# Inputs of head pairs 2 and 3 loaded ahead of the weights, and new operation lengths in a kernel's own list scheduler

## The chip, the core and the metric

The kernel runs on one core of one Trainium2 chip. The core has five engines with their own instruction queues: TensorE (PE; its weight loads are listed apart as PEld), VectorE (DVE), ScalarE (ACT), GpSimd (POOL) and SyncE (SP). SP computes nothing here; it issues nearly all DMA transfers. The metric is the device time of one launch in microseconds (us); lower is better. The median of three runs of the kernel before is 600.06 us (597.63 to 600.74).

## The reference

Gated linear attention (a state per head, decayed by alpha and fed by k and v, read by q), then the real part of a 2D Fourier transform of the result, added to it, then a layer norm and a feed-forward layer of ReLU type. The weights come as float64, the rest as float32. Cut to what matters:

```python
# q, k, v, alpha: (4, 8, 768, 48), alpha in 0.8 .. 1.0
for t in range(768):
    state = alpha[:, :, t, :, None] * state + np.einsum('bhd,bhe->bhde', k[:, :, t], v[:, :, t])
    y[:, :, t] = np.einsum('bhd,bhde->bhe', q[:, :, t], state)
x = y.transpose(0, 2, 1, 3).reshape(4, 768, 384)
u = x + np.real(np.fft.fft(np.fft.fft(x, axis=1), axis=2))
un = (u - u.mean(-1, keepdims=True)) / np.sqrt(u.var(-1, keepdims=True) + 1e-6)
out = u + np.maximum(un @ w_ch1, 0.0) @ w_ch2      # w_ch1 (384, 1536), w_ch2 (1536, 384)
```

## The kernel before

**Work and stages.** There are 4 batches (b = 0 to 3) of 4 head pairs, so 16 pairs, counted 0 to 15 in the code and in this text. For each batch there is a front (attention of its four pairs, then mixing) and a feed-forward part over two blocks of 384 tokens.

Attention of a pair is `attn_stages` (L609), stages s1 to s7 and a last one. s1 takes the products of the decays: `products` (L615) runs two scans of 112 x 768 elements on DVE over the tile `al` (alpha), with a few tiny operations between them: a copy of every 64th decay into `d1` (trace: COPY d<-al), a reciprocal, a copy of reciprocals into `d1` (COPY d<-rec), and the product `mt`. s2 and s3 multiply by k and q out of the tile `kq` (`times`, L643, on DVE or POOL). s4 transposes k (PE) into `kt`; s5 (pairs 0 to 6, float32) or s5r (from pair 7, in split float32r, tiles `qs`) makes the masked products of q and k (PE, ACT; the mask is an affine_select on POOL, tile `w`); s6 makes the states `tt` (PE, ACT, two DVE scans of 288); s7 makes y out of the masked products, `vn` (v) and `tt` on PE. The last stage is `combine` (L766): sums and differences of halves and thirds of the sequence, on POOL, with two steps on DVE.

Mixing is `mix_stages` (L783): `f2` (L799) folds the 384 columns on DVE, with nine tiny column copies per batch (COPY w<-x or w<-w, 128 x 2 or 4; each on the flexible list 'fc', which names DVE alone); then two rounds of Fourier matmuls (`mk_s`, `mk_d`) with additions on DVE. `norm_stages` (L887) normalises and transposes a block. `ffn_stages` (L935) is the feed-forward part: for each block 12 steps, each with 9 matmuls of 128 x 384 to the hidden layer and 9 back; ACT and DVE split each hidden tile `h` between them. In the trace these matmuls are f<-x,wt and f<-wt,h; there are 1728 of them, 432 per batch.

**Weights.** float64 weights come in four groups g of three tiles `wt0` to `wt11` (`load_weights`, L577, four DMAs each). `wsplit` (L588) turns a tile into a high and a low float32r part, with DVE, ACT and POOL steps; 12 splits in all. Feed-forward of batch 0 walks the weights in parts of 6, 3 and 3 steps (groups 0 and 1, then 2, then 3).

**The order.** The program writes instructions down with a key each, and `Plan.emit` (L331) gives every engine a fixed order by list scheduling: at each step it takes, over all engines, the instruction that can start first by the plan's own clock, and among those of an engine that could start within a small window the one with the lowest key. The lengths that this clock uses come from `duration` (L289). An operation with a flexible engine list (L447: 'mul' is DVE or POOL, and so on) goes to the engine that ends it first, with some slack (L446). The hardware then runs each engine's list in that order; an engine whose next instruction is not ready waits, whatever else would be ready behind it. Keys: batch 0's attention from -600 (`order`, `front` L1012), its weights' splits KW = -505 and KW1 = -260, later splits KW2 = 515, mixing of batch 0 KF0 = -505, attention of batch 1 K1 = 515, feed-forward 500 up.

**Transfers.** All SP loads keep program order (`self.chain` in `add`). A load whose tile is still in use holds the SP queue. `kq` and `vn` have two tiles each (NQK, NVN, L39 and L40), `al` has four (NAL). `load_first` brings pair 0, then come pair 1 (L1088 on) and a second copy of pair 0's alpha for the range check (`check_first`); alpha of pair p + 2 is issued behind s1 of pair p (`front`), k, q and v of pair p + 2 behind s7 of pair p. The weight groups are issued behind the units of `order` counted by LG = (8, 22, 40, 52), the Fourier constants `cst` behind unit L1 = 35. PE runs filler matmuls on a tile of zeros (trace: f<-zero, L1099) in gaps that the plan sees in its first 120 us.

Of the kernel before, what the change touches and what calls it, by code (L numbers as in the profile page):

```python
# [26 lines left out]
C = 64  # L27
# [15 lines left out]
KW = -505.0  # L43
LG = (8, 22, 40, 52)
L1 = 35
MIX = (5, 2, 2, 3, 3)
# [68 lines left out]
class View:  # L115
    """A tile of the plan, or a part of one: the steps are replayed on the real tile."""

# [18 lines left out]
class Slot:  # L136
    """One tile as the program sees it; it gets a real tile of its tag when its first instruction is placed."""

# [5 lines left out]
class Rows:  # L144
    """Row numbers of an indirect DMA."""

# [29 lines left out]
class Plan:  # L176
    """Instructions written down in program order, then given an order on every engine by list scheduling."""

# [37 lines left out]
    def add(self, engines, name, args, kwargs):  # L216
        engine = engines[0]
        fns = {e: self.method(e, name) for e in engines}
        if self.direct:
            return fns[engine](*[real(a) for a in args], **{k: real(x) for k, x in kwargs.items()})  # L220
        op = Op(engines, fns, args, kwargs, self.key)
        n = len(self.ops)
        self.ops.append(op)
        named = [("out" if i == 0 and "out" not in kwargs else i, a) for i, a in enumerate(args)] + list(kwargs.items())
        op.free, op.fill = 1, self.fill
        op.bytes = None
        for k, a in named:
            if isinstance(a, Rows):
                a = a.view
            if isinstance(a, View):  # L230
                self.touch(n, op, a, k in ("out", "accum_out"))
                if k == "out":
                    op.free = self.region(a)[4]
                if k == 2:
                    op.moving = a
        op.name = name
        named = dict((str(k), a) for k, a in named)
        op.durs = {e: self.duration(op, named, e) for e in engines}
        if engine == "SP" and isinstance(named["out"], View):
            if self.chain is not None and self.chain not in op.deps:  # L240
                op.behind = self.chain
                op.deps.add(self.chain)
            self.chain = n
        if "dma" in name:
            op.wire = self.wire(named)
# [43 lines left out]
    def duration(self, op, named, engine):  # L289
# [3 lines left out]
        if engine == "PE":  # L293
            m = self.region(named["1"])[4]
            if op.name == "transpose":
                return max(m, self.region(named["2"])[4]) / 1200 + 0.002
            if str(named["1"].real(self.base(named["1"])).dtype).endswith("float32"):
                return max(m, n) / 600 + 0.004
            return n / 2400 + 0.003
        if engine == "ACT":  # L300
            pointer = 0.094 if any(isinstance(named.get(k), View) for k in ("bias", "scale")) else 0.0
            return (0.05 if self.psum(named.get("1")) else 0.093) + n / 1200 + pointer + (0.096 if "accum_out" in named else 0.0)
        if op.name == "memset":
            return n / (960 if engine == "DVE" else 1100) + 0.01
        if engine == "DVE":
            if op.name == "bn_stats":
                return 0.47
            if op.name == "reciprocal":
                return 0.07 + n / 160
            if isinstance(named.get("scalar1"), View):  # L310
                return 0.07 + n / 1200
            whole = "bitcast" in [s[0] for s in named.get("out", View(None)).steps]
            pointer = 0.06 if isinstance(named.get("scalar"), View) else 0.0
            return 0.07 + pointer + n / (1920 if whole and op.name == "tensor_scalar" else 960)
        return 0.126 + n / 1094 if op.name == "affine_select" else 0.15 + n / 477

    def psum(self, view):
# [13 lines left out]
    def emit(self):  # L331
# [11 lines left out]
        dge, wire = 0.0, 0.0  # L343
        order = []

        def start(op, e):
# [14 lines left out]
        while placed < len(ops):  # L361
# [39 lines left out]
            if op.name == "matmul" and self.idle and (op.args[0].tile.tag, op.args[0].tile.cell) == self.idle[3]:  # L401
                self.open = not op.kwargs["stop"]
            end = t + op.dur
            clock[op.engine] = end
# [41 lines left out]
SLACK = {'ACT': 2.0, 'DVE': 0.5, 'POOL': 5.0}  # L446
FX = {'comb': 'G', 'mul': 'VG', 'first': 'G', 'wm': 'VG', 'wd': 'VG', 'fold': 'V', 'ev': 'A', 'relu': 'A', 'un': 'V', 'hi': 'A', 'xh': 'A', 'er': 'AV', 'fc': 'V', 'kl': 'V'}  # L447
WINDOW = {'PE': 0.0, 'ACT': 0.15, 'DVE': 0.05, 'POOL': 0.5, 'SP': 0.0, 'DMA': 0.0}
# [3 lines left out]
def gla_mix_ffn(ctx: ExitStack, tc: tile.TileContext, alpha, kq, v, w1, w2, consts, rowtab, out):  # L452
# [41 lines left out]
    def w3():  # L494
        return plan.tile("w3")

    def fixed(shape, name, dtype=F32):
        return plan.fixed(cp.tile(shape, dtype, name=name))

# [1 line left out]
    cst = fixed([P, CONST_W], "cst")  # L501
# [38 lines left out]
    def load_alpha(p):  # L540
        if p < B * NP2:
            t = plan.tile("al")
            loaded["al", p] = t
            SY.dma_start(t[0:CW, 0:S], alpha[p])

    def load_rest(p):
        if p < B * NP2:
            t, vn = plan.tile("kq"), plan.tile("vn")
            loaded["kq", p] = t
            loaded["vn", p] = vn  # L550
            SY.dma_start(t[0:CW], kq[p])
            SY.dma_start(vn, v[p])
# [54 lines left out]

# [1 line left out]
    def attn_stages(b, hp, i, mixed):  # L609
# [5 lines left out]
        def products(lo, hi):  # L615
            as_, Af, o = loaded["al", pair], e["A"], off(lo)
            d, chunks = d1[0:CW, lo:hi], slice(lo // C, hi // C)
            V.tensor_copy(d[:, 0::C], as_[0:CW, o : o + hi - lo : C])
            V.memset(as_[0:CW, o : o + hi - lo + 1 : C], 0.0)
# [5 lines left out]
            V.reciprocal(r, part[:, C - 1 :: C])  # L625
            V.tensor_copy(d[:, 2 * C - 1 :: 2 * C], r[:, 1::2])
            j0, j1 = max(lo // P - 1, 0), hi // P - 1
# [129 lines left out]

# [1 line left out]
    def early():  # L759
# [23 lines left out]
    def mix_stages(ytiles, zt, scr, us):  # L783
# [15 lines left out]
        def f2():  # L799
# [4 lines left out]
            for z, f in zip(zp, fp):  # L804
                ze, zo = f[:, :, 0 : HM + 1], f[:, :, HM:DM]
                E.tensor_add(ze[:, :, 1:HM], z[:, :, 1:HM], z[:, :, DM - 1 : HM : -1])
                FL["fc"].copy(ze[:, :, 0 : HM + 1 : HM], z[:, :, 0 : HM + 1 : HM])
                E.tensor_sub(zo[:, :, 1:HM], z[:, :, 1:HM], z[:, :, DM - 1 : HM : -1])
                g = [z[:, :, o : o + len(r)] for o, (r, _) in zip((0, HQ + 1, 2 * HQ + 1, 3 * HQ), GROUPS)]
                E.tensor_add(g[0][:, :, 0:HQ], ze[:, :, 0:HQ], ze[:, :, HM:HQ:-1])  # L810
                FL["fc"].copy(g[0][:, :, HQ : HQ + 1], ze[:, :, HQ : HQ + 1])
                E.tensor_sub(g[1][:, :, 0:HQ], ze[:, :, 0:HQ], ze[:, :, HM:HQ:-1])
                E.tensor_sub(g[2][:, :, 0 : HQ - 1], zo[:, :, 1:HQ], zo[:, :, HM - 1 : HQ : -1])
                E.tensor_add(g[3][:, :, 0 : HQ - 1], zo[:, :, 1:HQ], zo[:, :, HM - 1 : HQ : -1])
                FL["fc"].copy(g[3][:, :, HQ - 1 : HQ], zo[:, :, HQ : HQ + 1])
                for i in range(2):
# [67 lines left out]

# [1 line left out]
    def norm_stages(us, blk, res):  # L886
        e = {}  # L887

        def n1():
# [16 lines left out]
            if blk == 0:  # L906
                uw = [w3(), w3()]
                un = [uw[0][:, 0:DM], uw[0][:, DM:S], uw[1][:, 0:DM]]
# [22 lines left out]

# [1 line left out]
    def ffn_stages(us, blk, res, store, f0=0, f1=DFF // P):  # L933
# [56 lines left out]
    def batch(b):  # L990
# [5 lines left out]
        return mixed  # L996

    def front(b, us, ress):
        mixed = batch(b)
        sts = [attn_stages(b, hp, (b * NP2 + hp) % 2, mixed) for hp in range(NP2)]  # L1000

        def unit(hp, n):
            def f():
                if hp < NP2:
                    sts[hp][n]()
                    if n == 0:
                        load_alpha(b * NP2 + hp + 2)
# [4 lines left out]
        for hp in range(NP2):  # L1012
            order += [
                unit(hp, 3), unit(hp, 4), unit(hp + 2, 0), unit(hp, 5), unit(hp + 1, 1),
                unit(hp + 1, 2), unit(hp, 6), lambda hp=hp: load_rest(b * NP2 + hp + 2), unit(hp, 7),
            ]
# [19 lines left out]
    load_first()  # L1036
    load_alpha(1)
    load_rest(1)
    us, ress = [], [{}, {}]
    order, mixing = front(0, us, ress)  # L1040

    def extra(i):
        if i in LG:
            load_weights(LG.index(i))
        if i == L1:
            load_consts(1)

    plan.key = KCK
    check_first()
    write(order, -600.0, after=extra)  # L1050
    plan.key = KW
# [48 lines left out]
    with tc.manual_schedule():  # L1100
        plan.emit()
# [1 line left out]
    main_pool.close()  # L1103
# [101 lines left out]
def layout(q, k, v, alpha, moe_w_ch1, moe_w_ch2):  # L1205
    """The inputs as the launch takes them: heads in pairs with the features before the tokens, float64 as 8-byte words."""

# [18 lines left out]
def tokens(o):  # L1226
    """The blocks of the launch as the rows of the sequence: the second block holds the tokens from the end."""
    res = np.empty((B, S, DM), o.dtype)
# [19 lines left out]
```

## Time and profile before

| | before |
|---|---|
| median of three runs | 600.06 us (597.63 to 600.74) |
| the profiled execution, span from first to last instruction | 600.8 us |
| PE busy in the span | 543.5 us (90%) |
| DVE busy | 397.0 us (66%) |
| POOL busy | 214.1 us (36%) |
| ACT busy | 213.4 us (36%) |
| HBM traffic | 69 GB/s over the span |

The page gives no time of the profiled execution other than its span; it lies 0.7 us above the median and 0.1 us above the highest of the three runs, so that sums made in the trace can be set against the median directly. How to read it: a row of the timeline has start, length, engine, line, operation, tiles (out<-in), shapes, count, and in brackets the idle time before it and what ended that. Nearly all instructions have line L434, since `emit` records them; the tile names tell them apart. Tile numbers are left out, so `w` is any of the `w3` tiles, `x`, `h`, `qs`, `al` and `y` likewise. The windows view gives the busy time of each engine in a stretch, with the number of instructions, the clock granted to TensorE (1.00 is full speed) and the DMA rate.

### The profile page before, as it was taken

The numbers are of one execution on the slowest core, as the hardware profiler recorded it, in microseconds if no ns is written. First come the engines' busy times: TensorE is split into PE (matmuls) and PEld (weight loads), VectorE is DVE, ScalarE is ACT, GpSimd is POOL, SyncE is SP. The second block draws the span as 40 slices with busy tenths as digits, with TensorE's granted clock in tenths as the row PEclk, the third lists the DMA queues.
The fourth block names the chain that finished last, engine by engine and source line by source line (L and its number), as shares of the span: only waits on it lengthen the run. The fifth ranks groups of instructions, "written<-read, shape, count | busy, mean of one in ns | idle before, by whom it ended". The sixth has DMA issues, their size and how long they took to land. (4 is left out here: it accounts for less than half of the span.)

```text
span 600.8 us, 9105 instructions
## 1 busy us (share of the span) xinstructions
PE 543.5 (90%) x3470; PEld 523.2 (87%) x3470; DVE 397.0 (66%) x863; ACT 213.4 (36%) x442; POOL 214.1 (36%) x252
## 2 busy tenths in 40 slices
PE   7989588998779999787999989977999999999995
PEld 6878578897679998777999979977999999999995
DVE  7998999879955699896635991596635921412211
ACT  2657233575333313464622221444712121211110
POOL 3689794337526101395540040085740000000000
PEclk7568567689959999997979999987979999999999
DMA  8827291720014101143240110120010000100101
GB/s 219 280 74 278 67 321 50 247 67 0 2 35 130 48 0 41 44 130 92 67 140 6 40 47 0 41 67 21 1 55 26 33 8 1 40 1 1 40 1 44
DMA packets 16546, 42.16 MB, mean 70 GB/s; under 512 B 1904, under 2 KB 7088, under 8 KB 16496
## 3 DMA queue, kind: packets, MB, share of 16 engines
q1 hardware_dynamic: 15440, 39.08, 20.5%
q0 software_dynamic: 768, 2.36, 1.5%
q8 instruction: 29, 0.48, 0.4%
q14 instruction: 21, 0.17, 0.1%
q10 hardware_dynamic: 288, 0.07, 0.1%
HBM read 34.42 MB, written 7.08 MB: 69 GB/s over the span
## 5 line engine op out<-in xcount | busy, mean ns | idle before, releaser
L434 PE MATMUL f<-wt,h 128*128 128x384 f32 x864 | 179.5, 347 | 6.3 <-DVE h L434 3.3
L434 PE MATMUL f<-x,wt 128*128 128x384 f32 x864 | 179.7, 347 | 0.0
L434 PEld LDWEIGHTS f<-wt,h 128*128 128x128 f32 x864 | 154.2, 193 | 8.7 <-DVE h L434 4.5
L434 PEld LDWEIGHTS f<-x,wt 128*128 128x128 f32 x864 | 155.3, 193 | 0.6 <-issue 0.3
L434 DVE SCALAR_TENSOR_TENSOR h<-f,h 128x384 fp32r<-128x384 f32 x96 | 53.1, 553 | 128.9 <-ACT h L212 128.5
L212 ACT ACTIVATE h<-f 128x384 fp32r<-128x384 f32 x96 | 47.1, 491 | 192.4 <-PE f L434 181.4
L434 POOL TENSOR_SCALAR_AFFINE_SELECT w<-w 128x512 f32<-128x512 f32 (+1 forms) x64 | 48.8, 790 | 47.8 <-ACT w L434 47.8
L434 PEld LDWEIGHTS a<-vn,w 128*128 128x128 f32 x324 | 58.3, 251 | 7.4 <-POOL w L434 7.0
L434 PE MATMUL a<-vn,w 128*128 128x64 f32 x324 | 59.7, 326 | 5.4 <-POOL w L434 5.4
L434 POOL TENSOR_TENSOR sd<-y,y 128x288 f32<-128x288 f32 x32 | 30.8, 984 | 53.5 <-ACT y L434 52.3
L434 POOL TENSOR_TENSOR w<-w,rec 112x384 f32<-112x384 f32 (+1 forms) x17 | 17.8, 1049 | 87.2 <-DVE mt L434 83.2
L434 PE MATMUL a<-tt,w 112*128 112x96 f32 x134 | 40.5, 400 | 8.6 <-DVE tt L434 8.6
L434 DVE SCALAR_TENSOR_TENSOR qs<-w,hm,qs 112x384 fp32r<-112x384 f32 x36 | 24.7, 711 | 27.2 <-ACT qs L434 27.1
L434 ACT COPY w<-a 128x512 f32<-128x512 f32 (+6 forms) x58 | 25.9, 481 | 33.0 <-PE a L434 26.6
L434 DVE TENSOR_TENSOR_SCAN al<-al,d 112x768 f32<-112x768 f32 (+1 forms) x17 | 36.7, 2160 | 0.4
L434 DVE TENSOR_TENSOR y<-y,a 128x191 f32<-128x191 f32 (+2 forms) x96 | 28.7, 342 | 12.4 <-PE a L434 12.3
L434 PEld LDWEIGHTS a<-tt,w 112*128 112x128 f32 x134 | 28.0, 261 | 9.8 <-DVE tt L434 9.7
L434 PE MATMUL a<-qs,qs 112*128 112x256 f32 x162 | 31.6, 322 | 4.8 <-DVE qs L434 4.1
L434 POOL TENSOR_TENSOR w<-sd 128x96 f32<-128x96 f32 x64 | 35.7, 577 | 0.0
L434 PE MATMUL a<-cst,w 96*128 96x96 f32 (+10 forms) x267 | 33.7, 269 | 0.0
L434 PEld LDWEIGHTS a<-cst,w 128*96 128x96 f32 (+7 forms) x267 | 32.3, 169 | 0.9
L434 PEld LDWEIGHTS a<-qs,qs 112*128 112x128 f32 x162 | 26.1, 217 | 7.8 <-DVE qs L434 5.5
(124 smaller groups left out, 743.3 us busy)
## 6 DMA issues: line engine op xcount, KB each, us to landing
kq<-in_kq_dram SPq DMA_DIRECT2D x15, 672.0 KB, 7.5
wt<-in_w_dram SPq DMA_DIRECT2D x8, 768.0 KB, 9.6
al<-in_alpha_dram SPq DMA_DIRECT2D x15, 336.0 KB, 4.3
vn<-in_v_dram SPq DMA_DIRECT2D x16, 296.0 KB, 2.8
out_dram<-y SPq DMA_DIRECT2D x24, 192.0 KB, 1.9
wt<-in_w_dram SPq DMA_DIRECT2D x8, 384.0 KB, 6.3
scr<-y SPq DMA_DIRECT2D x4, 576.0 KB, 4.5
cst<-in_consts_dram SPq DMA_DIRECT2D x1, 832.5 KB, 5.2
```

Of the source, the lines that this page charges most:

```text
L212: return lambda out, x: e.activation(out, x, AF.Relu)
L434: op.ins = op.fns[op.engine](*[real(a) for a in op.args], **{k: real(x) for k, x in op.kwargs.items()})
```

## The change

Four things are changed.

1. Pairs 1, 2 and 3 (the second to the fourth) are loaded right behind pair 0: alpha, k and q, and v. k and q of pairs 2 and 3 go into the tiles `wt9` and `wt10`, v of both into `wt11`, which are those of weight group 3. Groups 0 and 1 and the Fourier constants are issued right behind, group 2 and 3 behind units 30 and 41 of the order. Behind pair 0 and 1 come k, q and v of pairs 4 and 5; from pair 4 on it is as before. Alpha of pair 4 on is issued from pair 2 on.
2. The lengths in `duration` are changed: longer for feed-forward matmuls, for strided float32 matmuls, for ACT, for the DVE scans; 0.02 us more for most DVE operations.
3. `emit` gets a model of DVE and POOL slowing each other: an operation with two wide SBUF inputs ("part") is lengthened by half of its overlap with the other engine's last operation, a tensor_scalar with fixed numbers ("whole") by all of it, and POOL's clock is pushed too.
4. The tiny copies in `products` and `f2` (70 in the trace before) become a DVE tensor_tensor, x or x on the bits (`same`). The normalised block 0 of batch 0 goes into two `qs` tiles instead of two `w3` tiles.

```diff
-LG = (8, 22, 40, 52)
-L1 = 35
+LG = (30, 41)
...
         op.durs = {e: self.duration(op, named, e) for e in engines}
+        op.port = self.port(op, named) if engine in ("DVE", "POOL") else None
...
             if str(named["1"].real(self.base(named["1"])).dtype).endswith("float32"):
-                return max(m, n) / 600 + 0.004
-            return n / 2400 + 0.003
+                slow = 1.65 if self.stride(named["2"]) > 16 else 1.0
+                return max(m, slow * n) / 600 + 0.004
+            return n / 2240 + 0.003
         if engine == "ACT":
             pointer = 0.094 if any(isinstance(named.get(k), View) for k in ("bias", "scale")) else 0.0
-            return (0.05 if self.psum(named.get("1")) else 0.093) + n / 1200 + pointer + (0.096 if "accum_out" in named else 0.0)
+            slow = 1.8 if self.stride(named["out"]) > 16 and n > 64 else 1.0
+            return (0.11 if self.psum(named.get("1")) else 0.14) + slow * n / 1200 + pointer + (0.25 if "accum_out" in named else 0.0)
...
+            if op.name == "tensor_tensor_scan":
+                return 0.1 + n / 480
             if isinstance(named.get("scalar1"), View):
-                return 0.07 + n / 1200
+                return 0.09 + n / 1200
...
-            return 0.07 + pointer + n / (1920 if whole and op.name == "tensor_scalar" else 960)
+            return 0.09 + pointer + n / (1920 if whole and op.name == "tensor_scalar" else 960)
...
+    def port(self, op, named):
+
+        if op.engine == "POOL":
+            return None if "dma" in op.name else "part"
+        if op.engine != "DVE" or op.name == "memset":
+            return None
+        inputs = [a for k, a in named.items() if k != "out" and isinstance(a, View)]
+        wide = [a for a in inputs if a.tile.tag not in ("a", "f1", "f2") and self.region(a)[4] > 1]
+        if len(wide) > 1:
+            return "part"
+        return "whole" if wide and op.name in ("tensor_scalar", "tensor_copy", "copy") and "scalar1" in named else None
...
+        held = {"DVE": (0.0, 0.0), "POOL": (0.0, 0.0)}
...
+            if op.port and op.engine in held:
+                other = "POOL" if op.engine == "DVE" else "DVE"
+                a, b = held[other]
+                both = max(0.0, min(b, t + op.dur) - max(a, t))
+                op.dur += (SHARE if op.port == "part" else 1.0) * both
+                if other == "POOL":
+                    clock[other] += SHARE * both
+                held[op.engine] = (t, t + op.dur)
...
+SHARE = 0.5
...
+    def same(out, x):
+        x = x.bitcast(I32)
+        V.tensor_tensor(out=out.bitcast(I32), in0=x, in1=x, op=ALU.bitwise_or)
...
+    def plain(t):
+        return t.rearrange("p c two n -> p (c two n)").bitcast(F32)
+
     def load_rest(p):
         if p < B * NP2:
-            t, vn = plan.tile("kq"), plan.tile("vn")
+            if p in (2, 3):
+                if p == 2:
+                    loaded["lent"] = plain(plan.tile("wt11"))
+                t = plain(plan.tile(f"wt{7 + p}")).rearrange("p (two s) -> p two s", two=2)
+                vn = loaded["lent"][:, (p - 2) * VW : (p - 1) * VW]
+            else:
+                t, vn = plan.tile("kq"), plan.tile("vn")
...
-            V.tensor_copy(d[:, 0::C], as_[0:CW, o : o + hi - lo : C])
+            same(d[:, 0::C], as_[0:CW, o : o + hi - lo : C])
...
-            V.tensor_copy(d[:, 2 * C - 1 :: 2 * C], r[:, 1::2])
+            same(d[:, 2 * C - 1 :: 2 * C], r[:, 1::2])
...
-                FL["fc"].copy(ze[:, :, 0 : HM + 1 : HM], z[:, :, 0 : HM + 1 : HM])
+                same(ze[:, :, 0 : HM + 1 : HM], z[:, :, 0 : HM + 1 : HM])
...
-                uw = [w3(), w3()]
+                uw = [plan.tile("qs").bitcast(F32) if state["start"] else w3() for _ in range(2)]
...
+    def rest_after(p):
+        if p < 2:
+            load_rest(p + 4)
+        elif p > 3:
+            load_rest(p + 2)
...
-                    if n == 0:
+                    if n == 0 and b * NP2 + hp > 1:
                         load_alpha(b * NP2 + hp + 2)
...
-    load_alpha(1)
-    load_rest(1)
+    for p in (1, 2, 3):
+        load_alpha(p)
+        load_rest(p)
...
     def extra(i):
         if i in LG:
-            load_weights(LG.index(i))
-        if i == L1:
-            load_consts(1)
+            load_weights(2 + LG.index(i))
...
+    plan.key = -600.0
+    load_weights(0)
+    load_consts(1)
+    load_weights(1)
     write(order, -600.0, after=extra)
```

More of the change, by code (lines that the diff above doesn't have):

```diff
@@ L309, in duration, with stride @@
                 return 0.07 + n / 160
+            if op.name == "tensor_tensor_scan":
+                return 0.1 + n / 480
             if isinstance(named.get("scalar1"), View):
-                return 0.07 + n / 1200
+                return 0.09 + n / 1200
             whole = "bitcast" in [s[0] for s in named.get("out", View(None)).steps]
             pointer = 0.06 if isinstance(named.get("scalar"), View) else 0.0
-            return 0.07 + pointer + n / (1920 if whole and op.name == "tensor_scalar" else 960)
+            return 0.09 + pointer + n / (1920 if whole and op.name == "tensor_scalar" else 960)
         return 0.126 + n / 1094 if op.name == "affine_select" else 0.15 + n / 477
+    def stride(self, view):
+        ap = view.real(self.base(view))
+        return abs(ap.ap[-1][0]) * mybir.dt.size(ap.dtype)
+    def port(self, op, named):
[8 more added lines that the diff above has]
+        return "whole" if wide and op.name in ("tensor_scalar", "tensor_copy", "copy") and "scalar1" in named else None
     def psum(self, view):
@@ L446 @@
 SLACK = {'ACT': 2.0, 'DVE': 0.5, 'POOL': 5.0}
-FX = {'comb': 'G', 'mul': 'VG', 'first': 'G', 'wm': 'VG', 'wd': 'VG', 'fold': 'V', 'ev': 'A', 'relu': 'A', 'un': 'V', 'hi': 'A', 'xh': 'A', 'er': 'AV', 'fc': 'V', 'kl': 'V'}
+FX = {'comb': 'G', 'mul': 'VG', 'first': 'G', 'wm': 'VG', 'wd': 'VG', 'fold': 'V', 'ev': 'A', 'relu': 'A', 'un': 'V', 'hi': 'A', 'xh': 'A', 'er': 'AV', 'kl': 'V'}
+SHARE = 0.5
 WINDOW = {'PE': 0.0, 'ACT': 0.15, 'DVE': 0.05, 'POOL': 0.5, 'SP': 0.0, 'DMA': 0.0}
@@ L810, in f2 @@
                 E.tensor_add(g[0][:, :, 0:HQ], ze[:, :, 0:HQ], ze[:, :, HM:HQ:-1])
-                FL["fc"].copy(g[0][:, :, HQ : HQ + 1], ze[:, :, HQ : HQ + 1])
+                same(g[0][:, :, HQ : HQ + 1], ze[:, :, HQ : HQ + 1])
                 E.tensor_sub(g[1][:, :, 0:HQ], ze[:, :, 0:HQ], ze[:, :, HM:HQ:-1])
@@ L814, in f2 @@
                 E.tensor_add(g[3][:, :, 0 : HQ - 1], zo[:, :, 1:HQ], zo[:, :, HM - 1 : HQ : -1])
-                FL["fc"].copy(g[3][:, :, HQ - 1 : HQ], zo[:, :, HQ : HQ + 1])
+                same(g[3][:, :, HQ - 1 : HQ], zo[:, :, HQ : HQ + 1])
                 for i in range(2):
@@ L1014, in front @@
                 unit(hp, 3), unit(hp, 4), unit(hp + 2, 0), unit(hp, 5), unit(hp + 1, 1),
-                unit(hp + 1, 2), unit(hp, 6), lambda hp=hp: load_rest(b * NP2 + hp + 2), unit(hp, 7),
+                unit(hp + 1, 2), unit(hp, 6), lambda hp=hp: rest_after(b * NP2 + hp), unit(hp, 7),
             ]
```

## The prediction

> **What bounds the kernel now.** I read the windows view first, with cuts at the start of the feed-forward part, at the end of the weight splits, and where DVE fills up again.
>
> ```profile
> core 0: us, PE busy (x) PEld busy (x) DVE busy (x) ACT busy (x) POOL busy (x), PEclk, DMA share, GB/s
> 0.00:119.88 119.88, 99.77 (x778) 91.99 (x779) 108.91 (x233) 55.56 (x111) 79.17 (x89) 0.68 0.62 193
> 119.88:172.00 52.12, 42.21 (x237) 39.48 (x236) 48.08 (x65) 27.37 (x46) 28.28 (x22) 0.89 0.06 20
> ...
> 234.00:280.00 46.00, 35.97 (x233) 32.38 (x232) 42.10 (x74) 22.03 (x49) 24.62 (x23) 0.97 0.22 65
> ...
> 119.88:593.20 473.32, 442.69 (x2690) 430.56 (x2690) 286.55 (x629) 157.84 (x331) 134.89 (x163) 0.94 0.13 39
> ```
>
> Two regimes are to be seen. Up to 172 us DVE is busy for 108.91 + 48.08 = 157 of 172 us (91%), so DVE sets the pace there; PE's busy time of the first stretch holds filler matmuls. From 119.88 on PE carries the feed-forward and what is left of attention and mixing. It loses 473.32 - 442.69 = 30.6 us idle, and at a mean clock of 0.94 another 0.06 x 473.32 = 28.4 us: 59 us that aren't work at full speed. In 234 to 280, with DVE 42.10 of 46 us busy, PE is idle for 10. The chain of waits, near the end of the run:
>
> ```profile
> 480.92 33.55 PE f L434 x192
> ```
>
> 192 matmuls in 33.55 us are 0.175 us each, back to back; nothing in this change makes one shorter. So only three things can move the end: DVE work up to 172 us, PE's idle time behind that, and the clock. What PE waits for from 119.88 on (total us, times, longest), the three largest rows:
>
> ```profile
> PE a L434 <- DVE tt L434: 7.1, 3, 3.3
> PE a L434 <- DVE al L434: 6.9, 2, 6.5
> PE a L434 <- DVE qs L434: 4.1, 3, 2.9
> ```
>
> These 18.1 of the 30.6 us (60%) are attention matmuls that stand in PE's fixed order ahead of their operands.
>
> **The change, part by part.** *Small copies.* Those up to 172 us, grouped by form, and a small product with two SBUF inputs of the same stage:
>
> ```profile
> L434 DVE COPY w<-x 128x2 f32<-128x2 f32 x6 | 5.8, 975 | 0.0
> L434 DVE COPY d<-al 112x12 f32<-112x12 f32 x8 | 3.8, 478 | 0.1
> L434 DVE TENSOR_TENSOR mt<-w 112x5 f32<-112x5 f32 x7 | 2.6, 370 | 0.0
> L434 DVE COPY d<-rec 112x6 f32<-112x6 f32 x7 | 1.2, 166 | 0.0
> L434 DVE COPY x<-w 128x4 f32<-128x4 f32 x3 | 1.1, 430 | 0.0
> L434 DVE TENSOR_TENSOR mt<-w 112x3 f32<-112x3 f32 x1 | 0.1, 127 | 0.0
> ```
>
> 24 copies take 5.8 + 3.8 + 1.2 + 1.1 = 11.9 us, although an undisturbed one takes 0.166 (third COPY row). One of them explains most of the first row:
>
> ```profile
> 87.05 5.07 DVE L434 COPY w<-x 128x2 f32<-128x2 f32 x1
> ```
> ```profile
> 86.45 1.12 POOL L434 DMA_INDIRECT y<-scr,rows  x1 [0.30 <-issue]
> ...
> 90.29 1.79 POOL L434 TENSOR_TENSOR w<-kq,w 112x768 f32<-112x768 f32 x1
> ```
>
> The copy ends at 92.12, when POOL's row of instructions without a gap, 7 from 86.45 on, ends (92.08): it got no turn between them. The replacement has two SBUF inputs, like mt. Its price lies between 0.127 us (undisturbed mt: 24 x 0.127 = 3.0, a gain of 8.9) and 0.370 us (mt in this stretch: 8.9, a gain of 3.0). I take 0.28, a little nearer mt's mean in this stretch, since it stands among the same operations: 6.7 us, a gain of **5.2**. It counts one for one, DVE being the bound here; the copy at 87.05 stands besides between the fold and the first Fourier matmuls. Behind 172 us:
>
> ```profile
> L434 DVE COPY d<-al 112x12 f32<-112x12 f32 x7 | 4.2, 607 | 0.1
> L434 DVE COPY d<-rec 112x6 f32<-112x6 f32 x8 | 3.0, 370 | 0.0
> L434 DVE COPY w<-w 128x2 f32<-128x2 f32 x18 | 2.9, 162 | 0.0
> ```
>
> The first two, 15 in 7.2 us, become 15 x 0.28 = 4.2: 3.0 us less on DVE, of which I count half, **1.5**, since only part stands in the stretches with DVE full. The fold copies aren't disturbed there (162 ns): between a gain of 0.04 and a loss of 0.1 us for each of the 18, taken as nothing.
>
> The Trainium skill, page "SBUF — State Buffer", section "Who interferes with whom", speaks against this part: it says that a DVE instruction with two SBUF inputs contends with a GpSimd instruction that reads SBUF as well, and that whoever comes second is blocked for the whole instruction. By that rule the sum here would be a gain of some 1 us instead of 5.2; mt's 370 ns agree with it in part, and no run here shows how the new form fares in the copies' places.
>
> *Early inputs.* What the SP queue did:
>
> ```profile
> 15.41 2.68 SPq L434 DMA_DIRECT2D wt<-in_w_dram  x4
> 18.18 1.40 SPq L434 DMA_DIRECT2D kq<-in_kq_dram  x1
> 30.63 0.38 SPq L434 DMA_DIRECT2D kq<-in_kq_dram  x1
> ```
>
> k and q of pair 2 are issued at 18.18, of pair 3 at 30.63, behind loads that wait for a tile. By the page's list of transfers:
>
> ```profile
> kq<-in_kq_dram SPq DMA_DIRECT2D x15, 672.0 KB, 7.5
> wt<-in_w_dram SPq DMA_DIRECT2D x8, 768.0 KB, 9.6
> al<-in_alpha_dram SPq DMA_DIRECT2D x15, 336.0 KB, 4.3
> vn<-in_v_dram SPq DMA_DIRECT2D x16, 296.0 KB, 2.8
> ...
> wt<-in_w_dram SPq DMA_DIRECT2D x8, 384.0 KB, 6.3
> ```
>
> Now 4 x (336 + 672 + 296) KB and 336 KB for the check go first, some 5.7 MB; at the 250 GB/s of the first 30 us that is 23 us, so pair 3 is in at about 25 instead of 38 (30.63 + 7.5), and the weights of group 0 (two of each wt size, 2.3 MB) at about 31, at a rate a little above that, instead of about 26:
>
> ```profile
> 0.00:30.00 30.00, 24.50 (x219) 22.24 (x219) 26.34 (x66) 14.46 (x28) 14.57 (x20) 0.63 0.88 250
> ```
> ```profile
> 26.28 0.56 DVE L434 TENSOR_SCALAR h<-wt 128x768 int32<-128x768 int32 x1
> 38.37 1.27 DVE L434 TENSOR_TENSOR al<-kq,al 112x768 f32<-112x768 f32 x1
> ```
>
> At 26.28 DVE began a split; pair 2's product came at 38.37, long after its data (18.18 + 7.5). Now the attention goes first and the split, not needed before 119.88, later. Work is swapped, not removed. What can be won is DVE's idle time, 119.88 - 108.91 = 11 us, less some 3 at the very start; what can be lost is 5 us of waiting for group 0, if nothing else were ready. Between +5 and -8 I take **-2**. Nothing is queued behind the new early loads that waited before; the later loads of pairs 4 and 5 wait for tiles of pairs 0 and 1 as those of 2 and 3 did, and group 3 waits until pair 3 is done with wt9 to wt11, well ahead of its use.
>
> *Lengths and port model.* The old lengths, beside what the trace shows:
>
> ```profile
> 99.69 1.76 DVE L434 TENSOR_TENSOR_SCAN al<-al,d 112x768 f32<-112x768 f32 x1
> 163.76 3.82 DVE L434 TENSOR_TENSOR_SCAN al<-al,d 112x768 f32<-112x768 f32 x1
> ```
> ```profile
> 119.88 3.55 PE L434 MATMUL f<-x,wt 128*128 128x384 f32 x10
> ...
> 161.70 0.76 PE L434 MATMUL f<-x,wt 128*128 128x384 f32 x3
> 168.97 0.79 PE L434 MATMUL a<-cst,al 112*128 112x112 f32 x3 [6.51 <-DVE al L434]
> 172.64 0.99 PE L434 MATMUL a<-vn,w 128*128 128x64 f32 x4
> 186.46 0.57 PE L434 MATMUL a<-vn,w 128*128 128x64 f32 x4
> ```
>
> The plan gave such a scan 0.07 + 768/960 = 0.87 us, the trace 1.76 alone and 3.82 beside POOL; the new length is 1.70, and overlap is added. A feed-forward matmul (the first is at 119.88) got 0.163, now 0.174, against 0.175. So the old plan placed attention matmuls too early: at 162.46 PE stops for 6.51 us, and then the same four matmuls take 0.99 instead of 0.57 us, so that the wait is paid again by a slow clock. The new plan should put feed-forward matmuls there. Bounds: nothing (DVE itself is 92% busy in 234 to 280, and PE can't be fed from nowhere), up to 60% of 59 us = 35 us, if every such wait and its clock went; below nothing, a new order makes waits of its own (a rival). I take a fifth of 59, **11.8** (60%, and a third of it), nearer the lower end, because where these waits stand DVE has 42.10 of 46 us filled.
>
> *The rest* (ACT lengths, strides, `qs` instead of `w3` for one block): no operation changes; their effect is part of the order above, and `qs` stays free until pair 7.
>
> Sum: 600.8 - 5.2 - 1.5 - 2 - 11.8 = **580.3 us**. The trace's span is 0.7 us above the median, within its spread, so I don't correct it.
>
> **The rivals.** *The new small operations are held up as the copies were*: for it stands mt's 370 ns beside 127. If each waits for POOL as the copy in its place did, only 0.166 - 0.127 = 0.04 us of each is won: 24 x 0.04 = 1.0 instead of 5.2, and 0.3 instead of 1.5; 580.3 + 4.2 + 1.2 = 586. *The order wins nothing*: the stretches stay DVE-bound, feed-forward moves into one wait and leaves another; for it stands DVE's 91%. 600.8 - 5.2 - 1.5 - 2 = 592. *The change doesn't do what it says*: what arrives earlier was never waited for, and copies and waits come back at other places; that no DMA is among the waits above speaks for it. About 600. *Slower*: feed-forward of batch 0 catches up with the weight splits. Its first part is 216 matmuls, 216 x 0.175 = 38 us; started at 112 and favoured over attention by the longer DVE lengths, PE would be at group 2 by 150 to 155. The last splits end here:
>
> ```profile
> 171.28 0.96 DVE L434 TENSOR_TENSOR wt<-w,wt 128x768 fp32r<-128x768 f32 x1
> ```
>
> If PE gets to a group before its split, it stops as at 162.46: 6.5 us and then half a clock for the 15 us or so between that wait and 180, 7.5 us more, 14 in all. With the gain by copies, 600.8 + 14 - 6.7 = 608. It decides when the first part ends over about 10 us ahead of group 2's splits; against it speaks that the plan knows the splits' lengths.
>
> **How the numbers follow.** Forecast, 570 to 592: 0.48. More than forecast, below 570: 0.10. Blocking like before, 586: 0.10. Order wins nothing, 592: 0.12. No change, 600: 0.09. Slower, 608: 0.11. A measurement of this kernel tells about 0.5% from no change, 3 us. Faster by over 0.5% (below 597): 0.48 + 0.10 + 0.10 + 0.10 of the 0.12 = 0.78; within: 0.11; slower: 0.11. The range runs from 563, into the case of more, to 602, which takes in no change; outside are 0.06 below and the slower case, 0.17 together.
>
> **What would show it.** Copies: no small DVE operation of 5 us; their groups near 0.28 us. Early inputs: no SP wait between the loads of pairs 1 to 3; products of pair 2 before 38 us, first split past 30. Order: first feed-forward matmul at 108 to 115 instead of 119.88; PE's waits on tt, al and qs well below 18 us, its mean clock behind that point above 0.94. It is wrong if PE's idle time and clock stay, or if waits on wt or h appear in their place.

## The result and the profile after

The changed kernel takes 579.33 us, the median of 4 runs (575.64 to 586.68), against 600.4 us for the kernel before in the same series (597.63 to 602.45): a ratio of **0.962 [0.958, 0.967]**, 3.8% faster. The ratios here and below leave out runs in a slow state, here the one of 586.68 us, so that they need not be the quotients of the medians. The profiled execution took 580.96 us, its span is 579.3 us: a run's time is 1.7 us longer than its span. So the span before, 600.8 us, belongs to the run of 602.45 us and not to one near the median. The spans differ by 21.5 us, as those two times do.

The page's totals of the kernel after:

```profile
span 579.3 us, 10236 instructions
PE 548.8 (95%) x4046; PEld 526.3 (91%) x4046; DVE 400.7 (69%) x860; ACT 212.9 (37%) x444; POOL 223.1 (39%) x253
```

DVE does 3.7 us more work than before (397.0), POOL 9.0 more (214.1). So the time didn't come from engine work that went away. The windows view says where it did come from: first the kernel before, cut at 172 us (where DVE's dense part ended) and at the end of PE's work, then the kernel after with the same first cut. The columns are those of the table in the prediction.

```profile
0.00:172.00 172.00, 141.97 (x1013) 131.47 (x1013) 156.99 (x297) 82.93 (x157) 107.45 (x111) 0.74 0.45 140
172.00:593.17 421.17, 400.45 (x2455) 391.05 (x2455) 238.45 (x564) 130.47 (x287) 106.61 (x141) 0.95 0.13 41
```
```profile
0.00:172.00 172.00, 157.10 (x1560) 143.90 (x1560) 147.05 (x280) 79.51 (x150) 96.81 (x104) 0.82 0.48 141
172.00:571.16 399.16, 390.69 (x2485) 381.74 (x2484) 252.09 (x579) 133.42 (x294) 126.25 (x149) 0.98 0.14 44
```

The work left for PE at 172 us, taken at full clock, is the same in both as far as a clock of two digits tells (some 2 us): 400.45 x 0.95 = 380 us before, 390.69 x 0.98 = 383 after. Before, it took 421.17 us; now it takes 399.16. **All 22 us are won behind 172 us, none ahead of it.** They are 12.2 us less idle time (421.17 - 400.45 = 20.7, now 8.5) and 13 us less lost by the clock (0.05 x 421 = 21, now 0.02 x 399 = 8), less 3 for the work. Ahead of 172 us DVE does 10 us less than before (147.05 instead of 156.99), and still the work left for PE at 172 us is the same.

What PE waited for from 100 us on (total us, times, longest), the four largest rows after:

```profile
PE a L464 <- POOL w L464: 3.7, 5, 1.5
PE a L464 <- DVE tt L464: 2.4, 4, 0.8
PE f L464 <- DVE qs L464: 2.4, 1, 2.4
PE a L464 <- DVE qs L464: 1.1, 2, 0.7
```

The waits of attention matmuls on `tt`, `al` and `qs` took 18.1 us before; 2.4 + 1.1 = 3.5 are left, with 2.4 more where another matmul waits on `qs`. No wait is longer than 2.4 us, where there was one of 6.5.

The timeline's rows that answer to those of the prediction: a kq load of SP, now into a `wt` tile, and the weights behind; on DVE the product of pair 2 and the first split; on PE the first feed-forward matmuls.

```profile
9.58 0.31 SPq L464 DMA_DIRECT2D wt<-in_kq_dram  x1
11.08 0.35 SPq L464 DMA_DIRECT2D wt<-in_v_dram  x1
...
15.21 6.09 SPq L464 DMA_DIRECT2D wt<-in_w_dram  x4
```
```profile
28.43 0.95 DVE L464 TENSOR_TENSOR al<-wt,al 112x768 f32<-112x768 f32 x1
...
30.54 0.56 DVE L464 TENSOR_SCALAR h<-wt 128x768 int32<-128x768 int32 x1 [1.14 <-DMA wt<-in_w_dram]
```
```profile
110.80 1.33 PE L464 MATMUL f<-x,wt 128*128 128x384 f32 x3
112.06 3.41 PE L1152 MATMUL f<-zero 128*32 128x32 f32 x60
...
129.24 1.85 PE L464 MATMUL f<-x,wt 128*128 128x384 f32 x9 [0.21 <-ACT w L464]
```

Pair 3's inputs are issued by 11.08 us, the product of pair 2 runs at 28.43 instead of 38.37, the first split at 30.54 instead of 26.28, and the feed-forward begins at 110.80. It begins with three matmuls, though: 60 fillers follow, and only 12 feed-forward matmuls start before 129.24. By 172 us 92 + 81 = 173 of the 1728 feed-forward matmuls are done, 181 before.

The small operations after, grouped by form over the whole run:

```profile
L464 DVE TENSOR_TENSOR d<-al 112x12 int32<-112x12 int32 x15 | 11.3, 754 | 0.1
L464 DVE TENSOR_TENSOR d<-rec 112x6 int32<-112x6 int32 x15 | 2.8, 188 | 0.1
L464 DVE TENSOR_TENSOR w<-w 128x2 int32<-128x2 int32 x18 | 2.8, 154 | 0.0
L464 DVE TENSOR_TENSOR w<-x 128x2 int32<-128x2 int32 x6 | 2.7, 444 | 0.0
```

One group went from 975 to 444 ns (w<-x), one from 538 to 754 (d<-al). All 70 small operations take 21.6 us, the copies took 24.1.

### The profile page after: what moved, and what is told of

It reads as the page before. It is cut to its first block, busy times and chain, and to the rows that moved or that the text cites. A ratio compares the mean times of both kernels' runs of the same rounds, so it can differ in the third digit from the quotient of the medians.

```text
span 579.3 us, 10236 instructions
## 1 busy us (share of the span) xinstructions
PE 548.8 (95%) x4046; PEld 526.3 (91%) x4046; DVE 400.7 (69%) x860; ACT 212.9 (37%) x444; POOL 223.1 (39%) x253
## 5 line engine op out<-in xcount | busy, mean ns | idle before, releaser
L464 PE MATMUL f<-x,wt 128*128 128x384 f32 x864 | 183.3, 346 | 0.2 <-ACT w L464 0.2
L464 PEld LDWEIGHTS f<-x,wt 128*128 128x128 f32 x864 | 153.4, 192 | 0.9 <-issue 0.3
L464 POOL TENSOR_TENSOR w<-w,rec 112x384 f32<-112x384 f32 (+1 forms) x17 | 23.2, 1363 | 107.0 <-DVE mt L464 66.0
L464 PEld LDWEIGHTS a<-vn,w 128*128 128x128 f32 x312 | 48.6, 214 | 5.5 <-POOL w L464 4.9
L464 PE MATMUL a<-vn,w 128*128 128x64 f32 x312 | 49.1, 287 | 3.7 <-POOL w L464 3.7
L1152 PEld LDWEIGHTS f<-zero 128*32 128x32 f32 x826 | 36.1, 130 | 7.1 <-issue 2.2
L1152 PE MATMUL f<-zero 128*32 128x32 f32 x826 | 40.5, 215 | 1.8 <-DVE zero L464 1.0
L464 PE MATMUL a<-tt,w 112*128 112x96 f32 x134 | 37.1, 372 | 2.5 <-DVE tt L464 2.4
L464 DVE TENSOR_TENSOR_SCAN tt<-us,seg 64x288 f32<-64x288 f32 (+1 forms) x32 | 32.8, 1025 | 6.8 <-ACT us L464 6.3
L464 DVE SCALAR_TENSOR_TENSOR qs<-w,hm,qs 112x384 fp32r<-112x384 f32 x36 | 28.8, 819 | 10.4 <-ACT qs L464 10.2
```

Source lines behind the costliest of these rows:

```text
L464: op.ins = op.fns[op.engine](*[real(a) for a in op.args], **{k: real(x) for k, x in op.kwargs.items()})
L1152: plan.idle = (lambda: nc.tensor.matmul(warm[2][0:32, 480:512], zero.real(), zero.real(), start=True, stop=True), 1.0, WARM, ("f2", 2))
```

## The experiments

Twelve kernels ran, each timed in three rounds beside the kernel before on the same chip (whose medians were 600.2 to 600.6 us). The move of one block to `qs` is in the change and in all kernels made from it, not in the `e` and `b` kernels.

| kernel | new copies' form | early inputs | lengths | port model, SHARE | median us | ratio to before |
|---|---|---|---|---|---|---|
| before | - | - | old | - | 600.4 | 1 |
| e1_copies | yes | - | old | - | 599.56 | 0.9955 [0.9904, 1.0006] |
| e2_loads | - | yes | old | - | 607.44 | 1.0128 [1.0079, 1.0178] |
| e3_lengths_port | - | - | new | 0.5 | 589.53 | 0.9835 [0.9780, 0.9889] |
| a1_copies_back | - | yes | new | 0.5 | 581.21 | 0.9673 [0.9617, 0.9729] |
| a3_old_lengths | yes | yes | old | 0.5 | 595.04 | 0.9851 [0.9802, 0.9900] |
| a4_no_port | yes | yes | new | none | 593.98 | 0.9901 [0.9864, 0.9937] |
| s03 | yes | yes | new | 0.3 | 590.10 | 0.9835 [0.9776, 0.9893] |
| the change | yes | yes | new | 0.5 | 579.33 | 0.9624 [0.9579, 0.9668] |
| a5_share07 | yes | yes | new | 0.7 | 561.68 | 0.9342 [0.9291, 0.9393] |
| s10 | yes | yes | new | 1.0 | 569.93 | 0.9473 [0.9426, 0.9520] |
| s07_old_loads | yes | - | new | 0.7 | 577.63 | 0.9620 [0.9578, 0.9662] |
| s07_jitter | yes | yes | new, +0.1 ns | 0.7 | 561.54 | 0.9376 [0.9332, 0.9419] |
| b1_jitter | - | - | old, +0.1 ns | - | 601.33 | 1.0008 [0.9973, 1.0042] |

**Copies.** `e1_copies` is the kernel before with the small copies replaced, and nothing else; the order of every engine stays.

```diff
-            V.tensor_copy(d[:, 0::C], as_[0:CW, o : o + hi - lo : C])
+            same(d[:, 0::C], as_[0:CW, o : o + hi - lo : C])
...
-                FL["fc"].copy(ze[:, :, 0 : HM + 1 : HM], z[:, :, 0 : HM + 1 : HM])
+                same(ze[:, :, 0 : HM + 1 : HM], z[:, :, 0 : HM + 1 : HM])
```

> The kernel before with the 70 small copies alone replaced by x or x on two SBUF inputs; the planned lengths of both forms are equal, so every engine keeps its order. Theory (copies worth 6.7 us as forecast): 593 to 594 us. Rival (the new form is held up by POOL as the copies were; the profile after has the alpha form at 754 ns against 538 of the copies before): 599 to 601, no change, with the 5 us hold at 87 us gone and others in its place.

`a1_copies_back` is the other side: the changed kernel with the copies as they were. The port model treats them there as it treats `same`, so that the order is again the changed kernel's on every engine.

```diff
-        if len(wide) > 1:
+        if len(wide) > 1 or wide and "copy" in op.name:
...
-            same(d[:, 0::C], as_[0:CW, o : o + hi - lo : C])
+            V.tensor_copy(d[:, 0::C], as_[0:CW, o : o + hi - lo : C])
```

> The changed kernel with the 70 small copies put back as tensor_copy, the plan told to treat them as before, so that every engine keeps the changed kernel's order. Theory (copies worth 5 to 7 us): 584 to 586. Rival (worth nothing): 578 to 581.

Groups by form, first of `e1_copies`, then of `a1_copies_back`:

```profile
L434 DVE TENSOR_TENSOR d<-al 112x12 int32<-112x12 int32 x15 | 8.2, 546 | 0.2
L434 DVE TENSOR_TENSOR w<-x 128x2 int32<-128x2 int32 x6 | 5.8, 971 | 0.0
L434 DVE TENSOR_TENSOR d<-rec 112x6 int32<-112x6 int32 x15 | 4.1, 272 | 0.1
```
```profile
L464 DVE COPY d<-al 112x12 f32<-112x12 f32 x15 | 9.1, 609 | 0.1
...
L464 DVE COPY w<-x 128x2 f32<-128x2 f32 x6 | 2.7, 450 | 0.0
```

In the copies' places the new form takes what the copies took: 971 ns where they took 975. And in the new order the copies take 450 ns where the new form takes 444. So the place decides far more than the form. (For d<-al the new form was longer than the copy in the same order, 754 against 609 ns, in one profiled execution each.) The one that stood for 5.07 us in the prediction stands again, though the rival had it gone, by the view of this tile between 75 and 100 us (shortest, median and longest in ns behind the count):

```profile
L434 DVE TENSOR_TENSOR w<-x x18: 148/344/5073, 82.8 to 93.3; 128x192 f32<-128x192 f32 x6, 128x2 int32<-128x2 int32 x6, 128x190 f32<-128x190 f32 x6
```

In time: 0.45% faster on the kernel before, with an interval that reaches past 1; 581.21 against 579.33 us in the change, with intervals that overlap. On the kernel before the new form is worth 2.7 us by the ratio (0.0045 x 600) and 0.8 by the medians (600.38 and 599.56), in the change 1.9 by the medians, and it can't be told from nothing.

`a1_copies_back` also shows how far one profiled execution can be trusted. Its profile is of its slowest run, 586.10 us, and by 172 us it has done 78 + 63 = 141 feed-forward matmuls, where the change with the same order has done 173. That delay stays to the end: the last row of 418 feed-forward matmuls on the critical chain, first of the change, then of `a1_copies_back`:

```profile
497.74 73.40 PE f L464 x418
```
```profile
502.95 73.40 PE f L464 x418
```

The difference is 5.2 us. Between `before`, `e1_copies` and `b1_jitter`, whose orders are the same but for a few rows, the same row differs by up to 5 us (519.78, 514.75 and 518.41). So a difference of 5 us between two single traces proves nothing about the kernels, and a delay ahead of 172 us does reach the end.

**Early inputs.** `e2_loads` is the kernel before with the new transfers only (all of part 1 of the change).

```diff
-LG = (8, 22, 40, 52)
+LG = (30, 41)
...
-    load_alpha(1)
-    load_rest(1)
+    for p in (1, 2, 3):
+        load_alpha(p)
+        load_rest(p)
```

> The kernel before with the new transfers alone (pairs 1 to 3 first, pairs 2 and 3 in tiles of the last weight group, weight groups as in the change), old lengths and old copies. Theory (the forecast's 2 us): 597 to 600. Rival (the early inputs are what starts the feed-forward earlier): 588 to 593, first feed-forward matmul at about 110 us.

It is 1.3% **slower**, outside both of its expectations. The inputs come as in the changed kernel, but this plan puts its first split at 41.67 us:

```profile
41.67 0.55 DVE L433 TENSOR_SCALAR h<-wt 128x768 int32<-128x768 int32 x1
```

Feed-forward begins at 124.99, 5.1 us later than before, 167 of its matmuls are done by 172 us instead of 181, and behind its start as much is lost as before, 27.8 us idle and 0.06 x 472.75 = 28.4 of clock:

```profile
124.99:597.74 472.75, 444.94 (x2694) 432.31 (x2693) 290.23 (x625) 158.43 (x333) 144.40 (x165) 0.94 0.12 39
```

The waits changed their names, not their sum. The three largest rows:

```profile
PE f L433 <- DVE h L433: 7.0, 5, 3.4
PE a L433 <- DVE tt L433: 6.5, 5, 2.5
PE a L433 <- DVE qs L433: 4.9, 5, 3.0
```

**Lengths and port model.** `e3_lengths_port` is the kernel before with parts 2 and 3 of the change: transfers and copies are the old ones.

```diff
+            if op.name == "tensor_tensor_scan":
+                return 0.1 + n / 480
...
+                op.dur += (SHARE if op.port == "part" else 1.0) * both
```

> The kernel before with the new lengths and the model of DVE and POOL slowing each other alone; old transfers, old copies. Theory (the order is the main term, larger than forecast, since PE's idle time and slow clock behind the start of the feed-forward fell from 59 to about 24 us): 575 to 585, PE waits on attention results below 8 us. Rival (lengths help only with the new transfers): 595 to 605.

1.7% faster, between its two expectations, and in an unexpected way. Feed-forward begins at 136.64 us, 16.8 us **later** than before, and the time is 11 us shorter. From the first feed-forward matmul on, and from 172 us on:

```profile
136.64:580.80 444.16, 427.18 (x2716) 415.80 (x2714) 295.17 (x627) 158.06 (x333) 146.72 (x165) 0.99 0.13 42
172.00:580.80 408.80, 393.04 (x2509) 383.04 (x2508) 265.62 (x587) 139.45 (x303) 133.24 (x154) 0.99 0.14 43
```

Idle are 444.16 - 427.18 = 17.0 us, and the clock costs 0.01 x 444 = 4.4: 21 us instead of 59. That stretch is shorter than the one before, though. By the cut at 172 us, which is the same for both, 15.8 + 4.1 = 20 us are lost instead of 42, with some 9 us more work left there (393.04 x 0.99 = 389 against 380). PE's waits on `tt` and `qs` come to 4.3 + 3.8 + 2.8 = 10.9 us, above the 8 expected, and still below the 18 of before. This is the mechanism of the change, and here it stands alone. It needs both halves, as the next two show, which take one half out of the changed kernel:

```diff
 a3_old_lengths: duration() as in the kernel before
-            if op.name == "tensor_tensor_scan":
-                return 0.1 + n / 480
 a4_no_port:
-            if op.port and op.engine in held:
+            if False:
```

> The changed kernel with the old lengths of PE, ACT, DVE and the scans; transfers, small operations and the port model as in the change. Theory (the lengths are what puts attention matmuls at the right place): 593 to 605 us, PE waits on attention results near those of before. Rival (the port model alone corrects the order): 580 to 586.

> The changed kernel with all new lengths, without the model of DVE and POOL slowing each other. Theory (lengths carry most, the port model a part): 583 to 590. Rival (the port model carries nothing): 577 to 582; rival (it carries most): 592 to 600.

Each takes away more than half of the gain: 595.04 (ten runs, 587.27 to 599.07) and 593.98 us. Without the port model feed-forward begins at 119.36, and 466.48 - 442.39 = 24.1 us idle and 0.04 x 466 = 18.7 of clock are lost behind it:

```profile
119.36:585.84 466.48, 442.39 (x2731) 429.70 (x2729) 304.68 (x636) 161.91 (x338) 154.78 (x171) 0.96 0.13 40
```

**How strong the port model is.** `s03`, `a5_share07` and `s10` change one number, the part of an overlap that the plan charges to an operation with two wide SBUF inputs and to POOL's clock: 0.3, 0.7 and 1.0 instead of 0.5.

```diff
-SHARE = 0.5
+SHARE = 0.7
```

> The changed kernel with SHARE at 0.7 instead of 0.5: a new order of the same kind. If the gain is in the kind of plan: 575 to 585. If it is the luck of one order: anywhere from 575 to 600.

> The changed kernel with SHARE at 0.3. If the time follows the nearness of the model: 582 to 592, between the 594 without the model and the 579 of 0.5. If orders scatter by luck: outside that, on either side.

> The changed kernel with SHARE at 1.0: an overlap with two wide SBUF inputs lengthens both operations by all of it. If the plan gains by coming nearer to what DVE and POOL do to each other, and they hold each other nearly whole: 555 to 565, at or below the 561.7 of 0.7. If the truth lies between 0.5 and 0.8: 565 to 580. If 0.7 was one lucky order: 575 to 595.

From no model over 0.3, 0.5 and 0.7 to 1.0 the medians are 594, 590, 579, 562 and 570 us. So 0.7 gives a kernel that beats the change as well, **6.6% faster than before** and below both of its expectations. Its stretch from the first feed-forward matmul on:

```profile
120.17:554.22 434.05, 424.85 (x2735) 414.52 (x2733) 298.39 (x638) 160.24 (x338) 161.40 (x169) 1.00 0.14 42
```

It begins 9 us later than the change, at the time of the kernel before, and ends 17 us earlier: 9.2 us are idle, and the clock costs nothing. 214 feed-forward matmuls are done by 172 us, against 173. Its three largest kinds of wait come to 1.6 to 2.3 us each:

```profile
PE a L464 <- DVE d L464: 2.3, 2, 1.6
PE f L464 <- DVE x L464: 1.8, 1, 1.8
PE a L464 <- DVE x L464: 1.6, 2, 1.3
```

**Is it the luck of one order?** A list scheduler can come to another order for any small change of a number. `b1_jitter` and `s07_jitter` make the planned feed-forward matmul 0.1 ns longer, in the kernel before and in the one with 0.7.

```diff
-            return n / 2240 + 0.003
+            return n / 2240 + 0.0031
```

> The kernel before with the planned length of a feed-forward matmul 0.1 ns longer, which changes nothing but the choice between near-equal orders. If the order of before is one of many alike: 597 to 604. If orders of this kind scatter widely, the time lies further off, and then single differences of under 1% between plans prove little.

> The kernel with SHARE at 0.7 and the planned feed-forward matmul 0.1 ns longer: a neighbouring order (about a quarter of PE's rows move). If 0.7 is better as a model: 558 to 568. If its order was luck: 570 to 590.

601.33 us instead of 600.6, and 561.54 instead of 561.68. In `b1_jitter` hardly anything moves, so that it says little; `s07_jitter` has another order (feed-forward begins at 112.46) and the same time. The steps between 0.5, 0.7 and 1.0 are 8 to 18 us, far above that. But this is one neighbour of one plan: none was run of the change or of `e2_loads`, so how much of their times belongs to their one order is open.

**Early inputs again, in the better plan.** `s07_old_loads` has SHARE = 0.7 and the transfers of the kernel before.

> The kernel with SHARE at 0.7 with the transfers of before (order of loads, tiles and weight groups as there). If the early inputs are worth the 8 us that they seem to bring at 0.5 (589.5 without, 581.2 with, both with the old copies): 567 to 573. If that difference was the order's and not the transfers': 557 to 565.

577.63 us, above both of its expectations: without the early inputs 16 us of the better plan are gone. `e3_lengths_port` and `a1_copies_back` show the same at 0.5, both with the old copies: 589.53 without the early inputs, 581.21 with them (and with the small move to `qs`, and with copies that the plan counts as two-input operations; neither was tried alone). Behind the start the loss is small without them too (436.63 - 424.95 = 11.7 us, clock 1.00), but the start is late:

```profile
132.18:568.81 436.63, 424.95 (x2712) 413.29 (x2713) 298.19 (x636) 160.82 (x338) 151.72 (x167) 1.00 0.13 42
```

## Why the prediction was right, and where it wasn't

The total, 580.3 us, lies 1 us from the median. That it came so near is in part luck: it is the sum of terms of which one was too small for the change and others too large, and it was counted from a span, so that as a time it would be 582. So each term has to be looked at. The row that answers to the prediction's cut, from the first feed-forward matmul on, of the kernel after, and one 20 us window of it:

```profile
110.80:571.16 460.36, 450.11 (x2920) 437.09 (x2919) 307.43 (x649) 166.28 (x351) 161.96 (x181) 0.97 0.14 43
...
240.00:260.00 20.00, 20.00 (x127) 19.62 (x126) 19.31 (x47) 8.50 (x20) 7.77 (x5) 1.00 0.08 31
```

- **The order (forecast 11.8 us): the mechanism was right, the size too small for the change.** Alone, in `e3_lengths_port`, it is worth 11 us, near the forecast; in the change, beside the early inputs, it is worth more. By the prediction's own cut the loss of 59 us fell to 10.25 idle (460.36 - 450.11) and 13.8 of clock (0.03 x 460), 24 us. That isn't 35 us of time, since PE's busy time there holds fillers until 129 us and more of the attention; by the cut at 172 us it is 25 of the 42 us lost. The step that failed is "I take a fifth of 59, 11.8 ..., because where these waits stand DVE has 42.10 of 46 us filled". A full DVE in one stretch was no limit: from 234 to 280 us DVE is busy for 43.53 of 46 us in the change (42.10 before), and PE for 43.65 (35.97 before). In the second row above, DVE is busy for 19.31 of 20 us and PE never idle. What PE needed was other work ready in its order, not more of DVE. `a5_share07` takes the loss to 9.2 us with as much DVE work behind the start as the change has, within 9 us. Less idle time came with a better clock, as the prediction had it, though not one for one: 17.0 us idle at 0.99 in `e3_lengths_port`, 10.25 at 0.97 in the change.
- **The bound up to 172 us didn't hold as a total.** "DVE sets the pace there", so that copies "count one for one", was the second base of the sum. The kernel after does 10 us less on DVE up to there and has the same work left for PE at 172 us; what moved back fits in behind, where DVE is 63% busy (252.09 of 399.16). A delay ahead of 172 us still costs time, as `a1_copies_back` shows against the change; that it is DVE's busy time which decides is what failed. Whether shorter copies would count one for one wasn't tested, since none of them got shorter at a fixed order.
- **Copies (5.2 + 1.5 us): mis-sized.** "I take 0.28, a little nearer mt's mean" failed: in the same place the operation takes the copy's time, 971 for 975 ns, and the rival that the new operations are held up as the copies were is what happened. Of its groups d<-al went to 754 ns. The two runs at fixed order leave 1 to 3 us of 6.7, not told from nothing. The Trainium skill, page "SBUF — State Buffer", section "Who interferes with whom", had this right: a DVE operation with two SBUF inputs contends with GpSimd too.
- **Early inputs (2 us): the sign depends on the plan.** Loads and first split came as forecast (by the 250 GB/s the 2.3 MB of group 0 take 9 us behind 25, so 34 and not 31; the first split needs only one of its tiles and began at 30.54). But "work is swapped, not removed" is no term that can be added. Alone they cost 7 us, behind the new lengths they bring 8, in the plan with 0.7 they bring 16. The bound of +5 was passed, the one of -8 as well.
- **The terms don't add.** By the medians, copies, early inputs, and lengths with port model are -1, +7 and -11 us each alone, a sum of -5; together they are -21. The prediction took them as a sum.
- **The signs.** All that was named for the order appeared: start at 110.80 (108 to 115 forecast), waits on `tt`, `al` and `qs` below 18 us, clock above 0.94. But the start of the feed-forward was no measure of the time: 110.80 gives 579 us, 120.17 gives 562, 136.64 gives 590. Only the loss behind the start together with the work done by then tells.
- **The slower rival** (feed-forward catching up with the splits) didn't come: no wait on `wt` is among the rows. What was slower, the early inputs in the old plan, was a case it didn't have.

Not settled: which of the new lengths matters (only all together were taken out); where between 0.5 and 1.0 the best SHARE lies, and whether 0.7 is nearest to what DVE and POOL do to each other, since only times were compared; and why the old plan with early inputs puts its first split at 41.67 us.

## What to carry to other kernels

Where a program orders its own instructions, the lengths it plans with are a part of the kernel: measure them in the trace, and model what two engines cost each other, before moving any work by hand. Test edits to such a kernel in the plan they will run in, since the same early loads were worth +7 us in one plan and -16 in another. In this kernel the time was won in the idle time and the clock behind the point where the long engine becomes the path, not in the busy time of the busiest engine ahead of it: look there first.

## What the runs showed of the hardware

- A DVE operation of 2 elements per partition stood for 5.07 us beside GpSimd, and again for 5.07 us with another opcode and two SBUF inputs.
- In the plan, 0.7 of the overlap gave the shortest time of the five values tried: 562 us, against 579 with half of it and 570 with all of it. By the Trainium skill, page "SBUF — State Buffer", section "Who interferes with whom", the ports that DVE shares with GpSimd are an exclusive lock, so that only the one that comes second would lose the overlap. The plan charges a DVE operation that meets one of POOL and pushes POOL's clock as well, so the five runs don't test that rule: they rank numbers to plan with, not what a single operation does.
- With PE idle for 9.2 of 434 us in short pieces, the granted clock was 1.00 behind the start; with 30.6 of 473, 0.94.
